# Heads and weight products as loops in a decode kernel (attention over a K/V cache, mixed with a gated MLP)

## The chip, the cores and the metric

One core of a Trainium2 chip. The metric is the device time of one execution in microseconds (us), lower is better. Engine names: PE is the matrix engine (PEld its weight loads), DVE the vector engine, ACT the scalar engine, POOL or GpSimd the general engine, SP the engine that issues the large transfers. PEldq, SPq and the like are rows of an engine's instruction queue: register, branch, semaphore and transfer-issuing instructions.

## The reference

All data is bfloat16. One token `x` (512 values) goes two ways, and a scalar gate mixes the results:

```python
x = A_x                                             # [1, 1, 512]
g = sigmoid((x * gate_w).sum(-1))
q = (x @ wq).reshape(32 heads, 128)                 # wq [512, 4096]
scores = einsum(q, k_cache) * 128 ** -0.5           # k_cache [1, 32, 65536, 128]
p = softmax(scores)
o = einsum(p, v_cache)                              # v_cache [1, 32, 65536, 128]
a = o.reshape(4096) @ wo                            # wo [4096, 512]
b = (silu(x @ w_gate) * (x @ w_up)) @ w_down        # F = 1792
out = g * a + (1 - g) * b
```

K and V are 2 x 32 x 16.8 MB; with the weights 1087.8 MB are read.

## The kernel before, in words

The program is written engine by engine: each engine's block is a list of instructions in program order, and semaphores tie the engines together (`wait_ge(s, n)` holds an engine until semaphore `s` has reached `n`). Nothing is planned at run time.

**Memory.** One large tile `mem` holds the weights, K and V in kilobyte places. Each half of a head's K or V (z = 0 or 1, 8.39 MB) has a fixed place; `load(kind, h, z)` fetches it with one transfer. Head 0's second K half takes the place of wq, so it waits for the last product with wq (`s_q`); the first two loads for head 1 and V of head 0 wait on `ktdone` (and `s_b`), which count transposes and the last product with w_down. SP issues all large transfers in program order on one queue.

**Start.** PE turns `x` into a column (`xTb`), multiplies it with wq for 32 heads (L446: four products of 128x128 weights per head, each with one column), then DVE and ACT spread q into `qd`, `qcur` and the gate into `gcol`. PE then forms gate and up (`mlp_up`, L474: 14 columns j, eight products each), ACT and DVE form `guT`, and PE starts `psY` with w_down (L482). DVE's first transposes (`transposes(0)`, L336) stand behind `guT` in its program, PE's first scores behind L482.

**Heads.** For each head DVE transposes K in 16 pieces into two buffers of `kt`; PE multiplies each with `qcur` (`scores`, L462) into `psS` and raises `qkdone`; a transpose waits until the piece two before it has been used. After the 16th, DVE takes the maximum, GpSimd reduces it over partitions (L280), ACT forms the exponentials (L305, L307) and copies the next head's query (L310), GpSimd sums (L282), DVE reorders them into `pb`, and PE multiplies with V (L515) during the next head, raising `pvdone`, which frees V's places for SP. `row_norm` on ACT scales the finished row and `turn` on PE stands it up as a column of `oTn`. PE and DVE run the heads as loops (`Fori`) already; PE's scores are inner loops (L508) whose output address `psS[:, ds(j * (2 * PR) + o, 4)]` is in a register. ACT, SP and GpSimd have the 32 heads written out.

**End.** The last V comes in eight pieces (`tail`), behind wo. PE multiplies the first piece (`piece(0)`, 128 rows), brings the first 31 heads' outputs into `oR` (L554), folds them with wo into `psY` (L559, 31 products), then does piece 1 (128 rows), the start of `psZ` (L567), pieces 2 to 7 (256 rows in all), and the last head's part of wo (L583). ACT copies the result (L314) and it is written out.

The lines of the products that the change turns into loops are

```python
last = nc.tensor.matmul(psM[:, 128 + h:129 + h], wq_ap[:, c, h * Dh:(h + 1) * Dh], xTb[:, c:c + 1], ...)
last = nc.tensor.matmul(psM[:, o + j:o + j + 1], w[:, c, :, j], xTb[:, c:c + 1], ...)
last = nc.tensor.matmul(psW[:, 0:1], vt[:, r * Dh:(r + 1) * Dh], pb[:, col:col + 1], ...)
last = nc.tensor.matmul(psY[0:1, :], oR[:, j:j + 1], wo_ap[:, j, :], start=False, stop=(j == 30))
```

Of the kernel before, what the change touches and what calls it, by code (L numbers as in the profile page):

```python
# [5 lines left out]
P = 128  # L6
# [9 lines left out]
ds = bass.DynSlice  # L16
# [5 lines left out]
def bass_gated_mix__mha_block_cached__swiglu_ffn__decode_kernel(  # L22
# [13 lines left out]
    _, H, S, Dh = A_k_cache.shape  # L36
    D = A_wq.shape[0]
    F = B_w_gate.shape[1]
    Dc = D // P
    FC = F // P  # L40
    R = S // P
    HR = R // 2
    NP = HR // PR
# [5 lines left out]
    KA, KZ, VA, VZ, V0 = 32, 0, 120, 96, 96  # L49
# [15 lines left out]
    with ExitStack() as ctx:  # L65
# [6 lines left out]
        def sem(name):  # L72
            return ctx.enter_context(nc.semaphore(name))
# [3 lines left out]
        psY = psum("psY", [P, 512], F32)  # L77
# [31 lines left out]
        def at(kb, n):  # L109
            return mem[:, kb * KB:kb * KB + n]  # L110
# [39 lines left out]
        pvdone = sem("pvdone")  # L150
        s_mx = sem("s_mx")
        s_ar = sem("s_ar")
        s_nb = sem("s_nb")
        expdone = sem("expdone")
        s_pba = sem("s_pba")
# [40 lines left out]

        def place(kind, h, z):
            if kind == "k":
                return (KA, V0)[z] if h == 0 else (KA, KZ)[z]
            return (VA, VZ)[z]  # L200

        def kv_dram(cache, h):
            return cache[0, h].rearrange("(b p r) d -> b p (r d)", b=2, p=P)

        for n, kb in (("wq", WQ), ("wg", WG), ("wu", WU), ("wd", WD)):
            src = w_dram[n]
# [7 lines left out]
        @block.sync  # L214
        def _(sp):
            def load(kind, h, z):
                cache = A_k_cache if kind == "k" else A_v_cache
                sp.dma_start(at(place(kind, h, z), HR * Dh), kv_dram(cache, h)[z]).then_inc(d[kind + "az"[z]], 16)

            half = HR // 2 * Dh  # L220
            for n in range(2):
                sp.dma_start(at(KA + 32 * n, half), kv_dram(A_k_cache, 0)[0][:, n * half:n * half + half]).then_inc(
                    (d["ka0"], d["ka"])[n], 16)
            sp.wait_ge(s_q, 1)
            load("k", 0, 1)
            for h in range(1, H):
                sp.wait_ge(ktdone, 2 * NP * h - 4 if h > 1 else NP)
                load("k", h, 0)
                if h == 1:
                    sp.wait_ge(ktdone, 2 * NP - 3)  # L230
                    sp.wait_ge(s_b, 1)
                else:
                    sp.wait_ge(pvdone, 4 * h - 1)
                load("v", h - 1, 0)
                sp.wait_ge(ktdone, 2 * NP * h + NP // 2)
                load("k", h, 1)
                sp.wait_ge(pvdone, 4 * h + 1)
                load("v", h - 1, 1)
            sp.wait_ge(ktdone, 2 * NP * H - NP)
            sp.dma_start(at(WO, 31 * D), w_dram["wo"][:, 0:31 * D]).then_inc(d["wo"], 16)  # L240
            src = A_v_cache[0, H - 1].rearrange("(b p r) d -> b p (r d)", b=2, p=P)
            need = {0: (ktdone, 2 * NP * H - 4), 1: (ktdone, 2 * NP * H), 2: (pvdone, 4 * H - 1)}
            for n, (kb, r0, nr) in enumerate(tail):
                if n in need:
                    sp.wait_ge(*need[n])
                b, o = divmod(r0, HR)
                sp.dma_start(at(kb, nr * Dh), src[b][:, o * Dh:(o + nr) * Dh]).then_inc(dt_[n], 16)  # L247
            sp.wait_ge(pvdone, 4 * H)
            sp.dma_start(at(WOJ, D), wj_dram).then_inc(d["wj"], 16)
            sp.dma_start(at(WO31, D), w31_dram).then_inc(d["w31"], 16)  # L250
            sp.wait_ge(s_fin, 1)
            sp.dma_start(out_dram[2:4, :], fin[32:34, :]).then_inc(s_out2, 16)

        @block.gpsimd
        def _(pool):
            nc.gpsimd.memset(onesf[0:1, :], 1.0)
            nc.gpsimd.memset(sel, 0.0).then_inc(s_sel0, 1)
            pool.wait_ge(s_sel0, 1)
            for je in range(4):
                off = 64 * (je // 2) + je % 2  # L260
                v = sel[:, je, :].rearrange("p (g d) -> p g d", g=4)
                last = nc.gpsimd.affine_select(out=v, in_=v, compare_op=ALU.not_equal, fill=1.0, base=-off,
                                               pattern=[[0, 4], [-2, 32]], channel_multiplier=1)
            last.then_inc(s_sel, 1)
            nc.gpsimd.memset(unit[:], 0.0).then_inc(s_unit0, 1)
            pool.wait_ge(s_unit0, 1)
            nc.gpsimd.affine_select(out=unit[:], in_=unit[:], compare_op=ALU.not_equal, fill=1.0, base=0,
                                    pattern=[[-1, 4]], channel_multiplier=1).then_inc(s_unit, 1)
            nc.gpsimd.memset(bmat[:], 0.0).then_inc(s_b0, 1)
            for q in range(4):  # L270
                pool.wait_ge(s_b0, q + 1)
                nc.gpsimd.affine_select(out=bmat[:], in_=bmat[:], compare_op=ALU.not_equal, fill=1.0, base=-32 * q,
                                        pattern=[[-1, 32]], channel_multiplier=1).then_inc(s_b0, 1)
            nc.gpsimd.memset(hot[0:1, :, :], 0.0).then_inc(s_hot0, 1)
            pool.wait_ge(s_hot0, 1)
            nc.gpsimd.affine_select(out=hot[0:1, :, :], in_=hot[0:1, :, :], compare_op=ALU.not_equal, fill=1.0,
                                    base=0, pattern=[[1, 2], [-1, 2]], channel_multiplier=0).then_inc(s_hot, 1)
            for h in range(H):
                pool.wait_ge(s_mx, h + 1)
                nc.gpsimd.partition_all_reduce(amx, mxs, P, RMAX).then_inc(s_ar, 1)  # L280
                pool.wait_ge(expdone, h + 1)
                nc.gpsimd.partition_all_reduce(Lt, rsum, P, RADD).then_inc(s_L, 1)  # L282

        @block.scalar
        def _(act):
# [8 lines left out]

            def row_norm(h):
                act.wait_ge(s_li, h + 1)
                act.wait_ge(pvdone, 4 * h + 8)
                act.wait_ge(s_pt, h + 1)
                nc.scalar.mul(orow[0:4, :], psO[0:4, :], Li[0:4, :]).then_inc(s_or, 1)  # L299
                act.wait_ge(s_pt, h + 2)  # L300
                nc.scalar.mul(oTn[:, h:h + 1], psT[:, 0:1], gcol[:, 0:1]).then_inc(s_otn, 1)  # L301

            for h in range(H):
                act.wait_ge(s_ar, h + 1)
                nc.scalar.mul(nbias, amx, -SCALE).then_inc(s_nb, 1)  # L305
                act.wait_ge(s_nb, h + 1)
                nc.scalar.activation(pa[:], psS[:], ACT.Exp, bias=nbias, scale=SCALE,  # L307
                                     accum_out=rsum).then_inc(expdone, 1)
                if h < H - 1:
                    nc.scalar.copy(qcur[:], qd[:, h + 1, :, :]).then_inc(s_qc, 1)  # L310
                if h >= 1:
                    row_norm(h - 1)
            act.wait_ge(s_z4, 1)
            nc.scalar.copy(fin[0:34, :], psZ[0:34, 0:128]).then_inc(s_fin, 1)  # L314
            act.wait_ge(s_fin, 1)
# [119 lines left out]
        def _(pe):  # L435
# [5 lines left out]
            last.then_inc(s_xT, 1)  # L441
            pe.wait_ge(s_xTb, 1)
            pe.wait_ge(d["wq"], 16)
            for h in range(H):
                for c in range(Dc):
                    last = nc.tensor.matmul(psM[:, 128 + h:129 + h], wq_ap[:, c, h * Dh:(h + 1) * Dh],  # L446
                                            xTb[:, c:c + 1], start=(c == 0), stop=(c == Dc - 1))
            last.then_inc(s_q, 1)
            pe.wait_ge(s_qTb, 1)
            pe.wait_ge(s_sel, 1)  # L450
# [16 lines left out]
            def mlp_up():  # L467
                pe.wait_ge(s_gc, 1)
                pe.wait_ge(d["wg"], 16)
                pe.wait_ge(d["wu"], 16)  # L470
                for j in range(FC):
                    for w, o in ((wg_ap, 64), (wu_ap, 80)):
                        for c in range(Dc):
                            last = nc.tensor.matmul(psM[:, o + j:o + j + 1], w[:, c, :, j], xTb[:, c:c + 1],  # L474
                                                    start=(c == 0), stop=(c == Dc - 1))
                last.then_inc(s_h, 1)

            mlp_up()
            pe.wait_ge(d["wd"], 16)
# [58 lines left out]
            def piece(n):  # L538
                kb, r0, nr = tail[n]
                pe.wait_ge(dt_[n], 16)  # L540
                vt = at(kb, nr * Dh)
                for r in range(nr):
                    col = k_col[r0 + r]
                    last = nc.tensor.matmul(psW[:, 0:1], vt[:, r * Dh:(r + 1) * Dh], pb[:, col:col + 1],  # L544
                                            start=(r0 + r == 0), stop=(r0 + r == R - 1))
                return last

            pe.wait_ge(s_or, H)
# [6 lines left out]
                             start=True, stop=True).then_inc(s_R, 1)  # L555
            pe.wait_ge(s_oR, 1)
            pe.wait_ge(d["wo"], 16)
            for j in range(31):
                last = nc.tensor.matmul(psY[0:1, :], oR[:, j:j + 1], wo_ap[:, j, :], start=False, stop=(j == 30))  # L559
            last.then_inc(s_y, 1)  # L560
            piece(1)
            pe.wait_ge(s_yr, 1)
# [51 lines left out]
```

## Time and profile before

| what | value |
|---|---|
| median of 3 runs (lowest, highest) | 2518.57 us (2518.57, 2519.21) |
| the profiled execution's own time | 2518.66 us |
| its span, first to last instruction | 2517.4 us |
| busy: PE, DVE, ACT, POOL | 67%, 56%, 3%, 1% |
| granted PE clock, mean | 0.71 of full speed |
| read from memory | 1087.77 MB, 432 GB/s over the span |
| instruction fetch in the page's queues q8 and q14 | 9 packets, 0.15 MB; 5 packets, 0.04 MB |

The page cuts the span into 40 slices; its row GB/s is what the transfers moved in each. The trace's timeline gives start, duration, engine, line, what is written from what, the count of merged instructions, and in brackets the idle time of the engine before them and what ended it. A source view gives, for one line, the durations (least, median, greatest, in ns) and the first and last start.

### The profile page before, as it was taken

How to read it: one execution, taken by the hardware profiler on the slowest of the kernel's cores; microseconds unless marked ns; L12 is line 12 of the kernel's file. 1: busy time of each engine (PE TensorE's matmuls, PEld its weight loads, DVE VectorE, ACT ScalarE, POOL GpSimd, SP SyncE). 2: the span in 40 equal slices, each digit the busy share in tenths (PEclk: the TensorE clock that was granted, in tenths of full speed). 3: DMA queues.
4: the chain of work that ended last, by engine and by line, in shares of the span. 5: the costliest groups of instructions: out<-in, count | busy, mean ns of one | idle time of the engine just before them, and what ended most of it. 6: DMA issues, size and time to landing. Idle time of an engine off the chain costs nothing.

```text
span 2517.4 us, 50622 instructions
## 1 busy us (share of the span) xinstructions
PE 1675.3 (67%) x21432; PEld 956.8 (38%) x21432; DVE 1397.7 (56%) x1631; ACT 65.6 (3%) x195; POOL 26.8 (1%) x83
## 2 busy tenths in 40 slices
PE   4566756667666577566676666766657756667667
PEld 3333333333433334333333333343333433333334
DVE  3764565554655645646456555465464564644653
ACT  0000000000000000000000000000000000000000
POOL 0000000000000000000000000000000000000000
PEclk8667767677677677676776767767767767677677
DMA  9999999999999999999999999999999999999999
GB/s 418 433 433 434 435 433 433 434 433 433 433 433 433 433 433 433 433 433 433 433 435 432 434 433 434 433 434 433 434 433 433 433 433 434 433 433 433 433 434 396
DMA packets 20474, 1087.97 MB, mean 432 GB/s; under 512 B 2282, under 2 KB 2668, under 8 KB 2924
## 3 DMA queue, kind: packets, MB, share of 16 engines
q1 hardware_dynamic: 20452, 1087.78, 99.9%
q8 instruction: 9, 0.15, 0.0%
q14 instruction: 5, 0.04, 0.0%
q10 hardware_dynamic: 8, 0.00, 0.0%
HBM read 1087.77 MB, written 0.00 MB: 432 GB/s over the span
## 4 chain that ended last, share of the span: by engine, by line
DMA 72%; PE 27%; DVE 0%; issue 0%; SPq 0%; ACT 0%
DMA mem<-in_A_v_cache_dram 70%; PE psO L515 27%; DMA mem<-in_A_k_cache_dram 2%; DMA mem<-in_A_wq_dram 1%; DVE kt L336 0%; PE psM L446 0%; SPq L247 0%; PE psZ L583 0%; PE psW L544 0%; ACT fin L314 0%
## 5 line engine op out<-in xcount | busy, mean ns | idle before, releaser
L462 PE MATMUL psS<-qcur,kt 128*128 128x4 bf16 x16384 | 573.7, 169 | 776.4 <-DVE kt L405 458.4
L515 PE MATMUL psO<-mem,pb 128*4 128x512 bf16 x3968 | 1033.6, 428 | 35.2 <-DMA mem<-in_A_v_cache_dram 35.2
L405 DVE STREAM_TRANSPOSE kt<-mem 128x2048 uint32<-128x2048 uint32 x248 | 551.2, 2280 | 571.9 <-DMA mem<-in_A_k_cache_dram 571.0
L462 PEld LDWEIGHTS psS<-qcur,kt 128*128 128x128 bf16 x16384 | 534.7, 106 | 852.4 <-issue 850.0
L412 DVE STREAM_TRANSPOSE kt<-mem 128x2048 uint32<-128x2048 uint32 x248 | 547.6, 2274 | 407.6 <-DMA mem<-in_A_k_cache_dram 407.6
L515 PEld LDWEIGHTS psO<-mem,pb 128*4 128x4 bf16 x3968 | 361.2, 93 | 666.2 <-issue 235.7
L345 DVE COPY pb<-pa 32x64 bf16<-32x64 bf16 x1024 | 233.5, 228 | 24.2 <-PE psO L515 9.5
L350 DVE TENSOR_REDUCE sm<-psS 128x1 f32<-128x512 f32 x32 | 22.1, 692 | 42.3 <-PE psS L462 42.3
L336 DVE STREAM_TRANSPOSE kt<-mem 128x2048 uint32<-128x2048 uint32 x16 | 35.4, 2277 | 16.9 <-DMA mem<-in_A_k_cache_dram 16.9
L280 POOL PARTITION_ALL_REDUCE sm<-sm x32 | 11.2, 351 | 2392.6 <-DVE sm L350 2392.6
L301 ACT ACTIVATE oTn<-psT,gcol 128x1 bf16<-128x1 f32 x31 | 8.2, 263 | 1063.2 <-PE psT L489 1063.2
L489 PE MATMUL psT<-unit,orow 4*128 4x1 f32 x256 | 33.5, 248 | 0.8 <-ACT orow L299 0.8
L299 ACT ACTIVATE orow<-psO,sm 4x512 f32<-4x512 f32 x31 | 21.0, 677 | 439.5 <-issue 439.5
L489 PEld LDWEIGHTS psT<-unit,orow 4*128 4x128 f32 x256 | 30.8, 186 | 1.9 <-ACT orow L299 1.3
L305 ACT ACTIVATE sm<-sm 128x1 f32<-128x1 f32 x32 | 6.5, 203 | 886.3 <-POOL sm L280 886.3
L307 ACT ACTIVATE pa<-psS,sm 128x512 bf16<-128x512 f32 x32 | 22.0, 687 | 1.0
L544 PE MATMUL psW<-pb,mem 128*128 128x1 bf16 x512 | 14.6, 165 | 7.6 <-DMA mem<-in_A_v_cache_dram 7.1
L544 PEld LDWEIGHTS psW<-pb,mem 128*128 128x128 bf16 x512 | 14.1, 102 | 8.7 <-issue 6.5
L282 POOL PARTITION_ALL_REDUCE sm<-sm x32 | 12.3, 383 | 36.4 <-ACT pa L307 36.4
L446 PE MATMUL psM<-xTb,mem 128*128 128x1 bf16 x128 | 3.6, 165 | 11.1 <-DMA mem<-in_A_wq_dram 11.1
L474 PE MATMUL psM<-xTb,mem 128*128 128x1 bf16 x112 | 6.9, 198 | 4.9 <-DMA mem<-in_B_w_up_dram 4.9
L432 DVE TENSOR_SCALAR w<-psW,sm 128x2 bf16<-128x2 f32 x1 | 0.2, 221 | 16.5 <-PE psW L544 16.5
(64 smaller groups left out, 63.1 us busy)
## 6 DMA issues: line engine op xcount, KB each, us to landing
mem<-in_A_v_cache_dram SPq DMA_DIRECT2D x3, 4096.0 KB, 29.4
mem<-in_A_k_cache_dram SPq DMA_DIRECT2D x2, 4096.0 KB, 38.8
mem<-in_A_wq_dram SPq DMA_DIRECT2D x1, 4096.0 KB, 12.6
mem<-in_A_wo_dram SPq DMA_DIRECT2D x1, 3968.0 KB, 37.0
mem<-in_A_v_cache_dram SPq DMA_DIRECT2D x1, 2048.0 KB, 32.9
mem<-in_B_w_gate_dram SPq DMA_DIRECT2D x1, 1792.0 KB, 16.4
mem<-in_B_w_up_dram SPq DMA_DIRECT2D x1, 1792.0 KB, 21.3
mem<-in_B_w_down_dram SPq DMA_DIRECT2D x1, 1792.0 KB, 25.1
```

Of the source, the lines that this page charges most:

```text
L282: nc.gpsimd.partition_all_reduce(Lt, rsum, P, RADD).then_inc(s_L, 1)
L299: nc.scalar.mul(orow[0:4, :], psO[0:4, :], Li[0:4, :]).then_inc(s_or, 1)
L307: nc.scalar.activation(pa[:], psS[:], ACT.Exp, bias=nbias, scale=SCALE, accum_out=rsum).then_inc(expdone, 1)
L336: nc.vector.transpose(kt[:, i % 2, :].rearrange("p (j r t) -> p r j t", j=2, t=32), src.rearrange("p (r j t) -> p r j t", j=2, t=32)).then ...
L345: last = nc.vector.tensor_copy(dst, sr)
L350: nc.vector.reduce_max(mxs, psS[:], AX_X).then_inc(s_mx, 1)
L405: nc.vector.transpose(kt[:, c % 2, :].rearrange("p (j r t) -> p r j t", j=2, t=32), src.rearrange("p (r j t) -> p r j t", j=2, t=32)).then ...
L412: nc.vector.transpose(kt[:, c % 2, :].rearrange("p (j r t) -> p r j t", j=2, t=32), src.rearrange("p (r j t) -> p r j t", j=2, t=32)).then ...
L462: last = nc.tensor.matmul(psS[:, o:o + 4] if j is None else psS[:, ds(j * (2 * PR) + o, 4)], ktb[b][:, je // 2, r, :, je % 2], qcur[:, je, ...
L489: last = nc.tensor.matmul(psT[:, 0:1], orow[0:4, i * Dh:(i + 1) * Dh], unit[0:4, i:i + 1], start=(i == 0), stop=(i == 3))
L515: last = nc.tensor.matmul(psO[0:4, :], pb[:, k_col[256 * z + r]:k_col[256 * z + r] + 4], vt[:, r * Dh:(r + 4) * Dh], start=(z == 0 and par ...
L544: last = nc.tensor.matmul(psW[:, 0:1], vt[:, r * Dh:(r + 1) * Dh], pb[:, col:col + 1], start=(r0 + r == 0), stop=(r0 + r == R - 1))
```

## The change

The 32 heads of SP, ACT and GpSimd, which were written out, become hardware loops: SP keeps head 1's loads and loops over 30 heads; ACT keeps the first exponentials and the last head and loops over 30; GpSimd loops over all 32, with an increment of a new semaphore `s_pool` between each wait and its reduction. K and V are then addressed in memory by a register. On PE four groups of products become loops: wq (7 turns of 4 heads, 4 heads written out), gate and up (13 turns of one column, the last written out), the first piece of the last V (8 rows written out, 15 turns of 8), and the fold with wo (5 turns of 5, 6 written out). In these loops the addresses of weights, columns and outputs come from registers (`ds(...)`). No product, transfer or buffer is added or left out.

```diff
         def kv_dram(cache, h):
-            return cache[0, h].rearrange("(b p r) d -> b p (r d)", b=2, p=P)
+            if isinstance(h, int):
+                return cache[0, h].rearrange("(b p r) d -> b p (r d)", b=2, p=P)
+            return cache[0, ds(h, 1)].rearrange("a (b p r) d -> b (a p) (r d)", b=2, p=P)
...
-            for h in range(1, H):
-                sp.wait_ge(ktdone, 2 * NP * h - 4 if h > 1 else NP)
-                load("k", h, 0)
-                if h == 1:
-                    sp.wait_ge(ktdone, 2 * NP - 3)
-                    sp.wait_ge(s_b, 1)
-                else:
-                    sp.wait_ge(pvdone, 4 * h - 1)
-                load("v", h - 1, 0)
-                sp.wait_ge(ktdone, 2 * NP * h + NP // 2)
-                load("k", h, 1)
-                sp.wait_ge(pvdone, 4 * h + 1)
-                load("v", h - 1, 1)
+            sp.wait_ge(ktdone, NP)
+            load("k", 1, 0)
+            sp.wait_ge(ktdone, 2 * NP - 3)
+            sp.wait_ge(s_b, 1)
+            load("v", 0, 0)
+            sp.wait_ge(ktdone, 2 * NP + NP // 2)
+            load("k", 1, 1)
+            sp.wait_ge(pvdone, 5)
+            load("v", 0, 1)
+            with nc.sync.Fori(0, H - 2) as i:
+                sp.wait_ge(ktdone, i * (2 * NP) + (4 * NP - 4))
+                load("k", i + 2, 0)
+                sp.wait_ge(pvdone, i * 4 + 7)
+                load("v", i + 1, 0)
+                sp.wait_ge(ktdone, i * (2 * NP) + (4 * NP + NP // 2))
+                load("k", i + 2, 1)
+                sp.wait_ge(pvdone, i * 4 + 9)
+                load("v", i + 1, 1)
...
-            for h in range(H):
+            with nc.gpsimd.Fori(0, H) as h:
                 pool.wait_ge(s_mx, h + 1)
+                nc.gpsimd.sem_inc(s_pool, 1)
                 nc.gpsimd.partition_all_reduce(amx, mxs, P, RMAX).then_inc(s_ar, 1)
                 pool.wait_ge(expdone, h + 1)
+                nc.gpsimd.sem_inc(s_pool, 1)
                 nc.gpsimd.partition_all_reduce(Lt, rsum, P, RADD).then_inc(s_L, 1)
...
-                nc.scalar.mul(oTn[:, h:h + 1], psT[:, 0:1], gcol[:, 0:1]).then_inc(s_otn, 1)
-
-            for h in range(H):
+                nc.scalar.mul(oTn[:, ds(h, 1)], psT[:, 0:1], gcol[:, 0:1]).then_inc(s_otn, 1)
+
+            def exps(h):
                 act.wait_ge(s_ar, h + 1)
...
-                if h < H - 1:
-                    nc.scalar.copy(qcur[:], qd[:, h + 1, :, :]).then_inc(s_qc, 1)
-                if h >= 1:
-                    row_norm(h - 1)
+
+            exps(0)
+            nc.scalar.copy(qcur[:], qd[:, 1, :, :]).then_inc(s_qc, 1)
+            with nc.scalar.Fori(0, H - 2) as i:
+                exps(i + 1)
+                nc.scalar.copy(qcur[:], qd[:, ds(i + 2, 1), :, :].rearrange("p a e g -> p (a e) g")).then_inc(s_qc, 1)
+                row_norm(i)
+            exps(H - 1)
+            row_norm(H - 2)
...
-            for h in range(H):
+
+            def project(h):
                 for c in range(Dc):
-                    last = nc.tensor.matmul(psM[:, 128 + h:129 + h], wq_ap[:, c, h * Dh:(h + 1) * Dh],
+                    last = nc.tensor.matmul(psM[:, ds(h + 128, 1)], wq_ap[:, c, ds(h * Dh, Dh)],
                                             xTb[:, c:c + 1], start=(c == 0), stop=(c == Dc - 1))
+                return last
+
+            with nc.tensor.Fori(0, (H - 4) // 4) as i:
+                for h in range(4):
+                    project(i * 4 + h)
+            for h in range(H - 4, H):
+                last = project(h)
...
-                for j in range(FC):
+                def up(j):
                     for w, o in ((wg_ap, 64), (wu_ap, 80)):
                         for c in range(Dc):
-                            last = nc.tensor.matmul(psM[:, o + j:o + j + 1], w[:, c, :, j], xTb[:, c:c + 1],
-                                                    start=(c == 0), stop=(c == Dc - 1))
-                last.then_inc(s_h, 1)
+                            last = nc.tensor.matmul(psM[:, ds(j + o, 1)],
+                                                    w[:, c, :, ds(j, 1)].rearrange("p m a -> p (m a)"),
+                                                    xTb[:, c:c + 1], start=(c == 0), stop=(c == Dc - 1))
+                    return last
+
+                with nc.tensor.Fori(0, FC - 1) as j:
+                    up(j)
+                up(FC - 1).then_inc(s_h, 1)
...
+                def row(r, col):
+                    return nc.tensor.matmul(psW[:, 0:1], vt[:, ds(r * Dh, Dh)], pb[:, ds(col, 1)],
...
+                if n == 0:
+                    first = 8
+                    for r in range(first):
+                        row(r, k_col[r])
+                    with nc.tensor.Fori(0, nr // 8 - 1) as i:
+                        for r in range(8):
+                            row(i * 8 + (first + r), i * 8 + (first + r))
+                    return
                 for r in range(nr):
-                    col = k_col[r0 + r]
...
+                    last = row(r, k_col[r0 + r])
                 return last
...
-            for j in range(31):
-                last = nc.tensor.matmul(psY[0:1, :], oR[:, j:j + 1], wo_ap[:, j, :], start=False, stop=(j == 30))
+
+            def fold(j, stop):
+                return nc.tensor.matmul(psY[0:1, :], oR[:, ds(j, 1)],
+                                        wo_ap[:, ds(j, 1), :].rearrange("p a n -> p (a n)"), start=False, stop=stop)
+
+            with nc.tensor.Fori(0, 5) as i:
+                for j in range(5):
+                    fold(i * 5 + j, False)
+            for j in range(25, 31):
+                last = fold(j, j == 30)
             last.then_inc(s_y, 1)
```

## The prediction

> **What bounds the kernel now.** I read the page first, for what is full.
>
> ```profile
> span 2517.4 us, 50622 instructions
> ...
> GB/s 418 433 433 434 435 433 433 434 433 433 433 433 433 433 433 433 433 433 433 433 435 432 434 433 434 433 434 433 434 433 433 433 433 434 433 433 433 433 434 396
> ...
> q1 hardware_dynamic: 20452, 1087.78, 99.9%
> ```
>
> One queue keeps 16 DMA engines busy for 99.9% of the span, at one rate; no compute engine passes 67% (PE). The trace's DMA records show the first packet at 1.75 us and the last input packet at 2514.81 us, with no hole between. So the bytes set the time, and an edit costs only if it empties that queue or lengthens what runs before the first or after the last byte. I therefore asked what covers each load: SP's line for the loads in the loop.
>
> ```profile
> L218 SPq DMA_DIRECT2D mem<-in_A_k_cache_dram x63: 327/328/328, 17.1 to 2417.0; - x63
> ...
> DMA to landing us min/median/max: 26.9/29.6/48.9
> ```
>
> A load is 8.39 MB: 19.4 us at 433 GB/s. The shortest way from issue to landing is 26.9, so at least 7.5 us of older work lies queued ahead of every load. That is the cover of the steady state. Next the two ends, by the timeline. The start, in three cuts of it (PE, DVE, SP's issue):
>
> ```profile
> 13.48 3.55 PE L446 MATMUL psM<-xTb,mem 128*128 128x1 bf16 x128 [11.10 <-DMA mem<-in_A_wq_dram]
> ...
> 23.04 6.85 PE L474 MATMUL psM<-xTb,mem 128*128 128x1 bf16 x112 [4.92 <-DMA mem<-in_B_w_up_dram]
> 31.42 5.02 PE L482 MATMUL psY<-mem,guT 128*1 128x512 bf16 x14 [1.53 <-DVE guT L389]
> ```
>
> ```profile
> 36.95 8.89 DVE L336 STREAM_TRANSPOSE kt<-mem 128x2048 uint32<-128x2048 uint32 x4 [5.67 <-DMA mem<-in_A_k_cache_dram]
> ...
> 66.00 11.08 DVE L336 STREAM_TRANSPOSE kt<-mem 128x2048 uint32<-128x2048 uint32 x5 [10.46 <-DMA mem<-in_A_k_cache_dram]
> ```
>
> ```profile
> 55.56 0.33 SPq L218 DMA_DIRECT2D mem<-in_A_k_cache_dram  x1
> ```
>
> And the end, PE alone:
>
> ```profile
> 2485.32 3.51 PE L544 MATMUL psW<-pb,mem 128*128 128x1 bf16 x128 [2.02 <-DMA mem<-in_A_v_cache_dram]
> ...
> 2489.16 8.61 PE L559 MATMUL psY<-mem,oR 128*1 128x512 bf16 x31 [0.28 <-DVE oR L426]
> 2497.71 3.36 PE L544 MATMUL psW<-pb,mem 128*128 128x1 bf16 x128
> ...
> 2504.77 3.55 PE L544 MATMUL psW<-pb,mem 128*128 128x1 bf16 x128 [3.17 <-DMA mem<-in_A_v_cache_dram]
> ```
>
> At the start DVE has 5.67 us to spare before its first transpose. The issue at 55.56 (k of head 1) waits for the eighth transpose (ktdone 8), and the queue is dry when the load before it lands at 66.0. At the end PE starts the last V's first piece when it lands (2485.3) and meets waits of a few us. What PE does from there in order, run end to end, is: 0.3 to the fold, 8.6, 3.3, 0.6 (L567), 3.5, then 124 products at 27 ns, 3.4: 19.7, with some 0.4 for its waits 20.1. The last V product now ends at 2514.93, so the first piece may last 2514.93 - 2485.3 - 20.1 = 9.5 us before the end moves; it lasts 3.5.
>
> **What a looped product costs.** PE already has such loops (L508, L462), and the trace has their register instructions:
>
> ```profile
> L462 PEldq FUSED_REGOPS  x3584: 46/46/65, 39.3 to 2465.4; - x200
> ```
>
> ```profile
> L508 PEldq COMPARE_BRANCH  x224: 76/208/243, 42.6 to 2465.6; - x112
> ```
>
> 3584 is a quarter of the 14,336 looped score products: each distinct register address takes one instruction, and the four products of a row share theirs. The new products share less: a row of the last V's piece has two addresses of its own (vt, pb), a head of wq has five (four weight slices, one output), one j of gate and up has ten. From the starts of records in the loop: a register instruction and its four weight loads and four matmuls take 124 ns; the first weight load starts 96 ns after the register instruction; two register instructions in a row are 99 ns apart (L508 to L501). So a product with one register instruction costs at least 46 + 2 x (124-46)/8 = 66 ns, at most 96 + 2 x 28/8 = 103 ns. I take 90, nearer the upper end, because that 96 ns is seen directly and how many of the 124 ns the eight others take is not. With two: 112 to 202; I take 99 + 90, 190 ns. An unlooped product: 27 ns (3.51/128). A loop's turn: increment to branch 93, branch to next instruction 267, that first register instruction 99: 0.46 us (0.36 if the last is counted among the addresses).
>
> **The change, part by part.** *The last V's first piece*: 8 unlooped rows 0.2, 120 rows x 0.19 = 22.8, 15 turns x 0.46 = 6.9: 29.9 us (19.0 to 33, the upper with 14 ns more for the longer address, by the 60 ns records of L462's first rows). Cover 9.5: the end moves by 20.4 (9.5 to 23.5). *Fold with wo*: five products take PE 5 x 0.278 = 1.39, the sequencer 5 x 0.19 + 0.46 = 1.41: hidden but for 0.1 (0 to 0.5 at 0.2 each). If PE's queue doesn't run ahead, 2 more.
>
> *wq*: 28 heads x (190 + 3 x 90 = 460 ns) = 12.9, 7 turns 3.2, four heads unlooped 0.4: 16.5 us (11.6 to 17.9) for 3.55. It ends at 30.0 (25.1 to 31.4). SP waits there on s_q to issue head 0's second K half: harmless, since the load ahead lands at 46.65 (DVE's wait on it ends there). DVE and ACT take 2.7 from s_q to gcol as before (17.06 to 19.73): PE is at gate and up at 32.7 (27.8 to 34.1), where it now comes at 23.04 by a DMA. *Gate and up*: one j is 2 x 460 = 920 ns plus 0.46; 13 of them 17.9, one unlooped 0.5: 18.4 us (13.2 to 19.8) for 6.85. Ends at 51.1 (41.0 to 53.9). guT follows 1.4 later, 52.5: past 36.95, so DVE's 5.67 us of cover is gone, its first transposes start there, and PE's 5.2 us of psY come before the first scores: 57.7, first group done at 58.9, when DVE may write kt again; six transposes at 2.22 follow: the eighth ends at 72.2 (62.1 to 75.0). SP's issue moves from 55.56 to there, bytes flow 1.0 later (first issue 0.72, first packet 1.75): the queue is dry from 66.0 to 73.2, **7.2 us** (0 to 10). What comes next is timed by landings and only shifts.
>
> *SP, ACT and GpSimd loops*: no loop of theirs is in this trace. PE's and DVE's register instructions (0.1 us apart) and turns are the nearest rows. Of what each repeats per head, the turn falls into long idle times (GpSimd's 75 us, ACT's 28 before L305), and the addresses between an SP wait and its issue, three or four, are 0.4 us; on SP the next load's wait is queued behind. ACT's chain (L305, L307) and GpSimd's two added semaphore steps together delay the exponentials by under 2 us; s_pool's increments stand behind waits that the reductions had before, with only the reduction behind them. All is under 7.5 us of cover: 0. *Instruction fetch*: the page's nine packets of q8 take 1.0 to 1.1 us each in the DMA records, q14's five in the span 0.31: 11 us of one engine, 0.7 us of sixteen. Perhaps a third goes: -0.3 (0 to -0.7).
>
> **Sum**, on the profiled execution's 2518.66 (span 2517.4 and 1.26 around it; 0.09 above the median): +20.4 +0.1 +7.2 -0.3 = 2546.1. Lower bounds together 2528, upper 2553.
>
> **Rivals.** *Not slower: register work costs a mere slot.* Place: the last V's piece. If an instruction costs the group's average, 124/9 = 13.8 ns, a row is 55 ns, the piece 0.2 + 6.6 + 6.9 = 13.7, 4.2 over its cover; wq then takes 8.7, gate and up 12.8 (the array's 61 ns a product hide the addresses), the eighth transpose ends near 59, no hole: 2522.6. It decides at (9.5 + 5.3 - 0.2 - 6.9)/120 = 64 ns a row for staying within 0.2%. For it: only 17 ns are lost per row of scores. Against: the 96 and 99 ns. Chance 0.10. The Trainium skill's "Runtime: NRT & Kernel Launch" (Instruction fetch mechanics) names one issue floor, about 20 cycles per instruction, which would favour this rival and its 2522.6; the trace's 99 ns between two register instructions speaks against applying it to them.
>
> *Every back edge refetches its code.* Forty new turns on PE, 20 at each end, at a packet's 1.05 us or more: 42 on top, 2588. Against: branch to next instruction is 265 to 312 ns in nine of ten of 160 inner turns, and q8 fetched nothing between 90 and 2491 us, with all of the heads' loops in between. 0.04. The same page and section has a taken branch outside a two-page window wait for a fetch, which is this rival's mechanism; here the bodies are short, and the trace shows it nowhere.
>
> *SP's, ACT's or GpSimd's loop eats more than 7.5 us per half head*: at 10, 2.5 x 30 or more, past 2593. Nothing in the profile is so slow. 0.03. *The loops end up without register work* (addresses folded): 2518.4. Two looped addresses cannot be constants; 0.03. *Faster*: needs 5 us of DMA time that no row offers; 0.02.
>
> **Numbers.** My sum holds 0.78. Range 2521 to 2558: from the slot rival's time past the upper bounds, with 5 us for the loops that no row shows. Slower by over 0.2% 0.85 (sum, refetch, slow loops), within 0.2% 0.13, faster 0.02; 0.2%, 5 us, is about what a measurement of this kernel can tell from no change.
>
> **What would show it.** Right: some 240 register instructions on the V piece's line and about 30 us of it from 2492 on (2485.3 plus the hole); no DMA wait of PE after that piece; the k issue of head 1 after 66 us and a lower second GB/s slice; q1's share below 99.9%; issue to landing still 27 us or more later. Wrong: the V piece under 15 us, k issued before 65, or holes in the DMA in the middle of the span.

## The result and the profile after

The changed kernel takes 2563.25 us (median of 6 runs, 2562.64 to 2563.88) against 2519.02: a ratio of 1.0176, interval 1.0166 to 1.0186, 44 us slower. The direction and the two places of the loss were forecast; the size was not: 2546 was said, with 2558 as the upper end.

The page of the changed kernel, the lines that answer to those of before:

```profile
span 2562.5 us, 52097 instructions
...
GB/s 413 328 426 437 431 434 434 434 434 434 433 434 434 433 435 432 435 432 436 431 437 428 440 428 440 428 438 430 437 431 437 431 436 432 435 433 434 434 429 213
...
q1 hardware_dynamic: 20452, 1087.78, 98.2%
q8 instruction: 7, 0.11, 0.0%
q14 instruction: 1, 0.01, 0.0%
```

The bytes are the same. Only the second slice (328 GB/s) and the last (213) have lost; from the third to the last but one the queue is as full as it was. So there is no loss per head. Each slice is 64 us: (433 - 328)/433 of it is 15.5 us, and (396 - 213)/433 is 27 us. In the DMA records the queue stands empty from 64.86 to 79.48 us, and the last input packet ends at 2532.1, 28 us before the last V product. The hole costs more than the 14.6 us in which all 16 engines stand still: their last packets before it end one after another, between 63.7 and 64.9 us, and in the first steps of 2 us after 80 us the queue moves 339 and 397 GB/s. By the bytes moved (at 27 MB) the changed kernel is then 16.1 us behind the kernel before.

The start, in the timelines of PE, DVE and SP (start us, us, engine, line, operation; in brackets the idle time before and its cause; "..." stands for lines left out):

```profile
14.13 2.52 PE L462 MATMUL psM<-xTb,mem 128*128 128x1 bf16 x16 [11.63 <-DMA mem<-in_A_wq_dram]
17.12 2.53 PE L462 MATMUL psM<-xTb,mem 128*128 128x1 bf16 x16 [0.48 <-issue]
...
31.98 3.19 PE L462 MATMUL psM<-xTb,mem 128*128 128x1 bf16 x32 [0.45 <-issue]
...
38.14 1.15 PE L497 MATMUL psM<-xTb,mem 128*128 128x1 bf16 x8 [1.88 <-ACT gcol L301]
39.60 1.17 PE L497 MATMUL psM<-xTb,mem 128*128 128x1 bf16 x8 [0.32 <-issue]
...
55.90 1.84 PE L497 MATMUL psM<-xTb,mem 128*128 128x1 bf16 x16 [0.31 <-issue]
59.27 5.03 PE L510 MATMUL psY<-mem,guT 128*1 128x512 bf16 x14 [1.53 <-DVE guT L404]
```

```profile
59.03 4.50 DVE L351 STREAM_TRANSPOSE kt<-mem 128x2048 uint32<-128x2048 uint32 x2
65.22 30.82 DVE L351 STREAM_TRANSPOSE kt<-mem 128x2048 uint32<-128x2048 uint32 x14 [1.69 <-PE psS L485]
```

```profile
78.52 0.33 SPq L221 DMA_DIRECT2D mem<-in_A_k_cache_dram  x1
```

wq's 128 products now take 21.0 us (14.13 to 35.17), one turn of four heads 2.99. Gate and up take 19.6 (38.14 to 57.74), one j 1.47. DVE's first transposes no longer wait for a DMA but for guT, the third waits for PE, and the issue for head 1's first K half, at 55.56 before, comes at 78.52, behind the eighth transpose.

The end, PE alone:

```profile
2502.36 2.31 PE L572 MATMUL psW<-pb,mem 128*128 128x1 bf16 x16 [1.74 <-DMA mem<-in_A_v_cache_dram]
2505.14 1.93 PE L572 MATMUL psW<-pb,mem 128*128 x8 [0.47 <-issue]
...
2536.71 1.92 PE L572 MATMUL psW<-pb,mem 128*128 x8 [0.46 <-issue]
2538.82 0.18 PE L595 MATMUL psQ<-bmat,amat 128*128 128x32 bf16 x1 [0.19 <-issue]
2539.60 9.27 PE L601 MATMUL psY<-mem,oR 128*1 x31 [0.59 <-DVE oR L441]
2548.80 3.41 PE L572 MATMUL psW<-pb,mem 128*128 128x1 bf16 x128
...
2553.08 6.99 PE L572 MATMUL psW<-pb,mem 128*128 128x1 bf16 x256
```

The first piece starts 17.0 us later than before and lasts 36.3 us (2502.36 to 2538.63) for 3.5. After it PE never waits for a DMA: all later pieces run in one row, x256. The last V product ends at 2560.07, 45.1 us later: 17.0 from the start, 26.8 by which the piece passes its cover of 9.5, and 1.3 in the fold, the pause before it and psZ.

What a looped row is made of is in the source view of the piece (durations least, median, greatest in ns):

```profile
L572 PEldq FUSED_REGOPS  x120: 46/74/84, 2502.6 to 2538.2; - x120
L572 PEldq ALU_OP  x105: 32/32/36, 2502.9 to 2538.4; - x105
```

Two register instructions a row, as assumed (FUSED_REGOPS and ALU_OP are both such; with 15 on the loop's own line L581 they are 240 for 120 rows). By the starts of records, the second follows 132 ns after the first, the weight load 60 later, the next row's first register instruction 53 after that: 245 ns a row. In wq's loop a product with one register instruction takes 124: 96 to its weight load, 28 or 29 on to the next. Gate and up is different from what was assumed:

```profile
L497 PEldq FUSED_REGOPS  x91: 46/46/79, 38.2 to 56.7; - x91
L502 PEldq FUSED_REGOPS  x13: 78/78/78, 38.0 to 55.8; - x13
```

That is 104 for 13 columns: eight register instructions a column, one for each product, where ten addresses had been counted. Some instructions last 78 or 79 ns instead of 46; the first product of each half, whose output address is new, has one of these and no second instruction.

### The profile page after: what moved, and what is told of

Read it like the earlier page. It is cut to its first block, busy times and chain, and to the rows that moved or that the text cites. A ratio compares the mean times of both kernels' runs of the same rounds, so it can differ in the third digit from the quotient of the medians.

```text
span 2562.5 us, 52097 instructions
## 1 busy us (share of the span) xinstructions
PE 1707.5 (67%) x21432; PEld 976.5 (38%) x21432; DVE 1397.3 (55%) x1631; ACT 65.6 (3%) x195; POOL 26.8 (1%) x83
## 4 chain that ended last, share of the span: by engine, by line
DMA 71%; DVE 14%; issue 10%; PE 4%; SPq 0%; DVEq 0%; ACT 0%; POOL 0%; ACTq 0%; POOLq 0%
DMA mem<-in_A_k_cache_dram 69%; DVE kt L420 7%; DVE kt L427 6%; PE psW L572 1%; DMA mem<-in_A_v_cache_dram 1%; DVE kt L351 1%; PE psO L543 1%; PE psM L462 1%; PE psM L497 1%; DMA mem<-in_A_wq_dram 1%; PE psY L601 0%; PE psS L485 0%; PE psY L510 0%; SPq L221 0%; DVE pb L360 0%
## 5 line engine op out<-in xcount | busy, mean ns | idle before, releaser
L485 PEld LDWEIGHTS psS<-qcur,kt 128*128 128x128 bf16 x16384 | 529.0, 105 | 849.3 <-issue 846.8
L572 PE MATMUL psW<-pb,mem 128*128 128x1 bf16 (+1 forms) x512 | 30.6, 165 | 17.8 <-issue 6.9
L289 POOL PARTITION_ALL_REDUCE sm<-sm x32 | 11.2, 351 | 2406.1 <-DVE sm L365 2313.5
L311 ACT ACTIVATE oTn<-psT,gcol 128x1 f32 (+1 forms) x31 | 8.2, 263 | 1070.0 <-PE psT L517 1070.0
L572 PEld LDWEIGHTS psW<-pb,mem 128*128 128x128 bf16 (+1 forms) x512 | 22.9, 102 | 26.2 <-issue 14.4
L462 PE MATMUL psM<-xTb,mem 128*128 128x1 bf16 x128 | 16.5, 181 | 16.2 <-DMA mem<-in_A_wq_dram 11.6
L462 PEld LDWEIGHTS psM<-xTb,mem 128*128 (+1 forms) x128 | 12.2, 104 | 20.5 <-issue 18.4
L497 PE MATMUL psM<-xTb,mem 128*128 128x1 bf16 x112 | 15.7, 216 | 5.8 <-issue 3.9
```

The costliest lines, as they stand in the source:

```text
L462: last = nc.tensor.matmul(psM[:, ds(h + 128, 1)], wq_ap[:, c, ds(h * Dh, Dh)], xTb[:, c:c + 1], start=(c == 0), stop=(c == Dc - 1))
L485: last = nc.tensor.matmul(psS[:, o:o + 4] if j is None else psS[:, ds(j * (2 * PR) + o, 4)], ktb[b][:, je // 2, r, :, je % 2], qcur[:, je, ...
L497: last = nc.tensor.matmul(psM[:, ds(j + o, 1)], w[:, c, :, ds(j, 1)].rearrange("p m a -> p (m a)"), xTb[:, c:c + 1], start=(c == 0), stop= ...
L572: return nc.tensor.matmul(psW[:, 0:1], vt[:, ds(r * Dh, Dh)], pb[:, ds(col, 1)], start=(isinstance(r, int) and r0 + r == 0), stop=(isinsta ...
```

## Experiments

All are edits of the changed kernel, against the kernel before in the same runs (2518.8 us). Theory A: the loss is what PE's register-addressed products take beyond their cover at the two ends. The rivals look for it in the other engines' loops, in code fetch, or in products and register instructions adding up.

**The V piece written out (x1_tail_plain).**

```diff
-                if n == 0:
+                if n < 0:
                     first = 8
```

> The changed kernel with the last V's first piece written out again (its 128 products as before); all other loops stay. Theory A (the loss is the price of register-addressed products at the two ends, 17.0 us at the start and 27 to 28 at the end): the start's 17.0 us stay, the end is back, 2519 + 17 = 2536 us (2535 to 2537.5), and the fold's loop stays hidden. Rival B (part of the loss comes from the loops of SP, ACT and GpSimd, such as GpSimd's first reduction, which starts 10.3 us after its wait): the start's share is theirs, the same 2536 here, but then the next run would not return to the time of before. Rival C (the end is late because code is fetched late after a loop, not because of the rows): the end would stay 3 us or more late, above 2539.

Measured: 2536.56 us (2536.30 to 2537.82), 17.7 over before. PE at the end:

```profile
2502.12 3.55 PE L572 MATMUL psW<-pb,mem 128*128 128x1 bf16 x128 [0.84 <-DMA mem<-in_A_v_cache_dram]
...
2506.32 9.63 PE L601 MATMUL psY<-mem,oR 128*1 x31 [0.60 <-DVE oR L441]
...
2521.70 3.39 PE L572 MATMUL psW<-pb,mem 128*128 128x1 bf16 x122 [0.35 <-DMA mem<-in_A_v_cache_dram]
```

The end is back to waits on the DMA, with the fold's loop in place. The DMA stands empty from 64.8 to 80.2 us, 15.4 us (14.6 in the full change). So 26.7 us of the 44 hang on this one loop; late code is not what holds the end.

**wq, gate and up written out (x2_start_plain).**

```diff
-            with nc.tensor.Fori(0, (H - 4) // 4) as i:
-                for h in range(4):
-                    project(i * 4 + h)
-            for h in range(H - 4, H):
+            for h in range(H):
                 last = project(h)
...
-                with nc.tensor.Fori(0, FC - 1) as j:
+                for j in range(FC - 1):
                     up(j)
```

> The changed kernel with wq's and gate's and up's products written out again; SP's, ACT's and GpSimd's loops, the V piece's loop and the fold's loop stay. Theory A: no hole in the DMA at the start; 2519 + 27.5 = 2546.5 us (2545.5 to 2548). Rival B: GpSimd's first reduction 10 us late holds the first loads of head 1 back: a hole of 2 to 10 us near 100 to 125 us, 2549 to 2557.

Measured: 2549.31 us (2548.42 to 2550.58). The hole at 65 us is gone, but the time lies 2.8 above theory A, in the rival's range. GpSimd's first reduction stands at 95.03 us (85.84 before) and the issue of head 1's second K half at 102.58 (94.52), as the rival has it. The queue is nowhere wholly empty, but it moves only 290 GB/s between 102 and 104 us and 172 between 124 and 126.

**All of PE written out (x3_pe_plain).** Both edits above, and the fold:

```diff
-            with nc.tensor.Fori(0, 5) as i:
-                for j in range(5):
-                    fold(i * 5 + j, False)
-            for j in range(25, 31):
+            for j in range(31):
                 last = fold(j, j == 30)
```

> All four groups of PE's products written out again; only the loops of SP, ACT and GpSimd stay. Theory A: they lie under the cover of the loads, 2519 us (2518 to 2520.5), at most 1 us for GpSimd's late first reduction. Rival B: 2521 to 2530, with a hole near 105 us or with issues of SP less than 19.4 us before landing.

Measured: 2523.17 us (2521.43 to 2526.39; ratio 1.0018, interval 1.0008 to 1.0027). Theory A fails here as it stood: the loops of SP, ACT and GpSimd are not free. The queue runs empty near 104.5 and 125.3 us, for 0.4 and 0.7 us; most of the loss is in the thin stretches around these moments. By the bytes moved the kernel is 2.0 us behind the kernel before after the first (at 45 MB) and 4.8 after the second (at 53 MB). The timelines of GpSimd, DVE and SP show from where; first the lines of the kernel before:

```profile
85.84 0.38 POOL L280 PARTITION_ALL_REDUCE sm<-sm  x1 [69.78 <-DVE sm L350]
```

```profile
94.52 0.33 SPq L218 DMA_DIRECT2D mem<-in_A_k_cache_dram  x1
```

And x3_pe_plain:

```profile
96.33 0.38 POOL L289 PARTITION_ALL_REDUCE sm<-sm  x1 [79.85 <-issue]
```

```profile
85.16 0.69 DVE L365 TENSOR_REDUCE sm<-psS 128x1 f32<-128x512 f32 x1 [1.34 <-PE psS L482]
85.76 4.50 DVE L420 STREAM_TRANSPOSE kt<-mem 128x2048 uint32<-128x2048 uint32 x2
99.34 4.51 DVE L420 STREAM_TRANSPOSE kt<-mem 128x2048 uint32<-128x2048 uint32 x2 [9.08 <-PE psS L482]
```

```profile
103.88 0.33 SPq L221 DMA_DIRECT2D mem<-in_A_k_cache_dram  x1
```

Head 0's maximum is ready at 85.85, but GpSimd reduces it at 96.33 (85.84 before). ACT's exponentials and its copy of head 1's query follow, PE's scores of head 1 wait for that copy, DVE's third transpose of head 1 waits 9.08 us for PE, and SP issues head 1's second K half at 103.88 instead of 94.52, when its cover is used up. GpSimd's row says "issue", not DVE: it was not waiting for the maximum any more. In the records its two MODIFY_POOL_CONFIG steps, which stood at 16.3 us before, now come right behind the wait (86.3 us here, the reduction 10.0 later; 98.5 and 10.3 in the full change). In the heads that follow, the reduction starts 0.2 to 0.3 us after its wait: the long gap is the first head's alone. What GpSimd does in it no record shows.

**The other half: PE's loops alone (x4_pe_loops).** SP, ACT and GpSimd as before.

```diff
-            with nc.gpsimd.Fori(0, H) as h:
+            for h in range(H):
                 pool.wait_ge(s_mx, h + 1)
-                nc.gpsimd.sem_inc(s_pool, 1)
                 nc.gpsimd.partition_all_reduce(amx, mxs, P, RMAX).then_inc(s_ar, 1)
...
-            with nc.sync.Fori(0, H - 2) as i:
+            for h in range(1, H):
...
-            with nc.scalar.Fori(0, H - 2) as i:
+            for h in range(H):
```

> The other half: SP, ACT and GpSimd written out as before, PE's four loops as in the change. Theory A: 2563 us (2561.5 to 2563.5). Rival B: 5 to 10 us less, 2553 to 2558, since the other engines' loops carry part of the loss.

Measured: 2562.21 us (2562.07 to 2563.34). Of the 44 us, 43 are PE's. The loops of the small engines cost 4.3 us alone (x3_pe_plain) and about 1 on top of PE's, by medians whose ranges of runs overlap: the 10 us of GpSimd's first reduction fall behind a start that is late already.

**One register address a row (x5_one_address).**

```diff
-                            row(i * 8 + (first + r), i * 8 + (first + r))
+                            row(i * 8 + (first + r), first + r)
```

> The changed kernel, but in the looped rows of the last V's piece the column of pb is a fixed one (the eight of the first eight rows, in every turn), so a row has one register address instead of two; the last head's product therefore weighs those rows wrongly. Theory A (each register instruction sets a fixed time, about 96 ns to the weight load and 28 more to the next register instruction): a row goes from 245 to about 140 ns, the piece from 36.5 to about 24.5 us, 2551 us (2549.5 to 2553). The prediction's price of 90 ns a row: 18 us for the piece, 2545 us.

Measured: 2551.53 us (2551.09 to 2551.81), 11.7 less than the full change. The source view and PE's timeline:

```profile
L572 PEldq FUSED_REGOPS  x105: 64/64/79, 2502.8 to 2526.6; - x105
```

```profile
2519.18 1.20 PE L572 MATMUL psW<-pb,mem 128*128 128x1 bf16 x8 [0.43 <-issue]
2520.85 1.18 PE L572 MATMUL psW<-pb,mem 128*128 128x1 bf16 x8 [0.47 <-issue]
```

A row takes 142 ns by the records and a turn of eight 1.63 to 1.67 us where it took 2.4; the piece ends at 2526.9. The prediction's price of 90 ns a row would have given 2545.

**Every looped product twice (x6_twice).**

```diff
                             row(i * 8 + (first + r), i * 8 + (first + r))
+                            row(i * 8 + (first + r), i * 8 + (first + r))
```

> The changed kernel with every looped product of the last V's piece issued twice with the same two register addresses (120 products more, the sum counts those rows twice). Theory A: the second product falls into the time that the register instructions take anyway: 0 to 0.5 us more, 2563 to 2564. The prediction's price (products and register instructions add up, 7 to 27 ns a product): 0.8 to 3.2 us more, 2564 to 2566.5.

Measured: 2563.87 us (2563.10 to 2564.47) beside 2563.25 (2562.64 to 2563.88): 0.6 more, the two ranges of runs overlap, and it lies just outside A's 0.5. The timeline decides it better:

```profile
2517.20 1.93 PE L572 MATMUL psW<-pb,mem 128*128 x16 [0.43 <-issue]
2519.56 1.97 PE L572 MATMUL psW<-pb,mem 128*128 x16 [0.43 <-issue]
2521.96 1.95 PE L572 MATMUL psW<-pb,mem 128*128 x16 [0.43 <-issue]
```

Sixteen products take the 2.4 us that eight took. By the starts of register instructions a row takes 254.8 ns in the mean, 254.6 in the changed kernel (the median is 245 in both). The second product fits beside the register instructions.

**Only wq's loop, or only gate's and up's (x7_wq_loop, x8_gate_loop).** Both keep the loops of SP, ACT and the fold, with GpSimd and the V piece written out.

```diff
-                if n == 0:
+                if n < 0:
...
-                with nc.tensor.Fori(0, FC - 1) as j:
+                for j in range(FC - 1):
                     up(j)
```

is x7; x8 has wq's loop written out in place of these last lines:

```diff
-            with nc.tensor.Fori(0, (H - 4) // 4) as i:
-                for h in range(4):
-                    project(i * 4 + h)
-            for h in range(H - 4, H):
+            for h in range(H):
                 last = project(h)
```

> Of PE's loops only wq's and the fold's stay (gate and up and the V piece written out), SP's and ACT's loops stay, GpSimd is written out. Theory A with covers: wq ends at 35.2, gate and up 38.1 to 45.0, guT 46.4, first scores at 51.7 to 52.9, the eighth transpose 13.3 later at 66.2, the first bytes at 67.2 to 67.3 against a queue that runs dry at 64.9: a hole of 2.3 us, 2521.3 us (2520.3 to 2522.5). Rival (each loop costs its share of the 17.0 us in proportion to the time that it adds, 17.5 of 30): 10 us, 2529.

> The same with gate's and up's loop instead of wq's. Theory A with covers: gate and up 23.0 to 42.6, guT 44.0, first scores at 49.3 to 50.5, the eighth transpose at 63.8, first bytes at 64.8 against a queue that runs dry at 64.9: no hole, 2519 us (2518.5 to 2519.8). Rival (proportional share, 12.8 of 30): 7 us, 2526.

Measured: wq alone 2521.73 us (2521.09 to 2522.30), gate and up alone 2520.35 (2519.21 to 2521.35; ratio 1.0006, interval 0.9996 to 1.0015). With wq's loop the issue stands at 65.98 us and the queue is empty from 65.56 to 66.94. The time lies in the range that was given, but with a hole of 1.4 us for the 2.3 expected, so the reckoning was right only in part. The time with gate's loop lies 0.5 us above its range. There the issue stands at 63.45, and the profiled execution (span 2518.4 us) has no moment at which all engines stand still; by the bytes moved it falls 1.1 us behind at this very place all the same (at 27 MB; with wq's loop 3.6). The sixteen shares of the older load end between 63.6 and 65.5 us, and between 64 and 67 us the queue moves 243, 358 and 360 GB/s. So "no hole" was not "no loss": the cover ends where the first engine runs out, here some 2 us before the last one does. Proportional shares (10 and 7 us) are excluded: 2.9 and 1.6 alone, 17 together.

**SP's and ACT's loops alone (x9_sp_act).** As x3_pe_plain, with GpSimd written out:

```diff
-            with nc.gpsimd.Fori(0, H) as h:
+            for h in range(H):
                 pool.wait_ge(s_mx, h + 1)
-                nc.gpsimd.sem_inc(s_pool, 1)
```

> Only SP's and ACT's loops stay; PE's four groups and GpSimd are written out as before. Theory A2 (what the three small engines' loops cost, 2.5 to 7.5 us, is GpSimd's alone: its wait is now an instruction of its own, the switch to the code of the reduction comes behind it instead of 70 us ahead, and the first reduction starts 10 us late): 2518.8 us (2518.4 to 2519.3), head 1's second K issue back from 103.9 to 94.5 us. Rival B2 (SP's or ACT's loop costs it): 2521 to 2524, as with all three.

Measured: 2518.75 us (2518.32 to 2519.36) beside 2518.80; ratio 1.0000, interval 0.9991 to 1.0009. The issue is back at 94.69.

**All three loops, GpSimd's first head taken out (x10_first_head_out).** An edit of x3_pe_plain.

```diff
-            with nc.gpsimd.Fori(0, H) as h:
+            pool.wait_ge(s_mx, 1)
+            nc.gpsimd.partition_all_reduce(amx, mxs, P, RMAX).then_inc(s_ar, 1)
+            pool.wait_ge(expdone, 1)
+            nc.gpsimd.partition_all_reduce(Lt, rsum, P, RADD).then_inc(s_L, 1)
+            with nc.gpsimd.Fori(1, H) as h:
```

> All three loops of SP, ACT and GpSimd stay, PE written out, but GpSimd's first head is taken out of its loop, with the waits on the reductions themselves as before. Theory A2: the switch happens early in the wait, 2518.8 us (2518.3 to 2519.3). Rival C2 (the added semaphore steps of every head cost it): 2521 to 2524 still. If the fetches of code that the loops save count (five of 0.3 us on one of 16 engines), it is at most 0.1 us under the kernel before, not measurable.

Measured: 2518.60 us (2518.30 to 2518.81); ratio 0.9999, interval 0.9990 to 1.0008. GpSimd's and SP's timelines:

```profile
85.96 0.38 POOL L287 PARTITION_ALL_REDUCE sm<-sm  x1 [68.74 <-DVE sm L369]
```

```profile
94.64 0.33 SPq L221 DMA_DIRECT2D mem<-in_A_k_cache_dram  x1
```

The first reduction is on time again, now released by DVE, and its two MODIFY_POOL_CONFIG steps stand at 17.4 us. So SP's, ACT's and GpSimd's loops cost nothing except through that first wait. Whether the separate wait or the added increment matters is not told apart: the two are one record, and every run has both or neither in the first head. No version beats the kernel before by more than the runs scatter.

## Why the prediction was wrong, point by point

**Right in mechanism:** the DMA queue bounds the time; the steady state covers the new loops of SP and ACT (least issue to landing 26.8 us with both loops alone, 26.7 with all three in x10; in the full change 22.9 among the early loads, 26.8 from 150 us on); the loss sits in a hole before head 1's first K half and in the last V's first piece; the fold hides. It took 0.66 us more than before, but its time goes with the granted clock of its stretch, looped or not: 8.36 us at 0.82 (x10) and 9.56 at 0.71 (x3) written out, 9.27 at 0.73 (full change) and 9.78 at 0.69 (x7) looped; time times clock is 6.7 to 6.9 us in each. Only the pause before it is longer with the loop, 0.6 us for 0.3.

**The term that failed: the price of a looped product.** The step took the 124 ns of a score group as one register instruction (46 ns by the lower bound, the 96 to the first weight load by the upper) plus eight others that share the rest, and gave a lone product two of the eight shares. They don't share it: the register instruction alone sets the 124. A second product beside it is free (x6), and without three others a lone product still takes 124. With one address a product takes 124 to 142, outside the bounds of 66 to 103; with two a row takes 245, outside 112 to 202. The upper bound was no bound, since it let the seven nanoseconds of two dispatched instructions stand for the whole way from the weight load to the next register instruction, which is 28 in the very records that were quoted, and took 99 ns between two register instructions where the longer ones of the new loops (74 to 79 ns each) are 132 to 137 apart.

| term | forecast | measured |
|---|---|---|
| row with two addresses, one address | 190, 90 ns | 245, 124 to 142 ns |
| V piece, end moved by it | 29.9, 20.4 us | 36.3, 26.8 us |
| fold, the pause before it and psZ | 0.1 us | 1.3 us |
| wq; a head of it | 16.5 us; 460 ns | 21.0 us; about 650 ns |
| gate and up; one j with its turn | 18.4, 1.38 us | 19.6, 1.47 us |
| register instructions in one j; ns for each | 10; 92 | 8; about 129 |
| eighth transpose and issue | 72.2 us | 78.5 us |
| hole in the DMA; the loss at the start | 7.2, 7.2 us | 14.6, 17.0 us |
| SP, ACT and GpSimd | 0 | 4.3 alone, about 1 here (within the 17.0) |
| instruction fetch | -0.3 us | not told apart from 0 (x10) |

The misses add up: 6.4 in the V piece, 1.2 around the fold, 9.8 at the start and 0.3 of fetch are 17.7, and the profiled execution (2563.88 us) lies 17.8 above the forecast of 2546.1. That one j of gate and up came near its forecast is luck: two register instructions too many were counted, each priced too low ((1.47 - 0.44)/8 = 0.129 us).

**The hole's edges** are a second, smaller miss: the queue was taken to run dry when the load's landing was seen before (66.0), but in the changed run its last packet ends at 64.86, so the hole is 1.1 us longer on that side. Part of this is the way from the last packet to the landing, 0.45 us in both runs (65.53 to 65.98 before, 64.86 to 65.31 in the changed run); why the load itself ends 0.7 us earlier stays open (in x7 it ends at 65.56). On top come the thin stretches on both sides of the hole. The cover of the steady state was taken too large too: of the 7.5 us, 1.0 go from issue to the first packet and 0.45 from the last packet to the landing, which leaves an estimated 6. The chain in between (guT, psY, first scores, six transposes at 2.2 us) ran as written; it began 0.65 us later, with wq's products.

**GpSimd** was put at 0 because its wait is long, and because "only the reduction" was said to stand behind the increments. What was missed is what else stands there: before, the wait was on the reduction, and the two MODIFY_POOL_CONFIG steps ran 70 us ahead; with the wait as an instruction of its own they run behind it, and the first reduction starts 10 us later. x3_pe_plain against x10_first_head_out shows what that costs: 4.6 us.

**The rivals:** the "mere slot" rival at 2522.6 needed 64 ns a row and is out by a factor of almost four. "Every back edge refetches" is out: the page shows seven packets on q8 for nine before, and a turn costs about 0.44 us over its rows (2.4 - 8 x 0.245). A slow loop of SP or ACT is out (x9). Loops without register work are out: the V piece has 240 register instructions.

## What to carry to other kernels

Price a looped product by its register instructions, read as the distance from one to the next in an existing loop of the same kind. Count how many addresses of its own each product has, and check the count in a trace where there is one: two addresses were two instructions in the V piece and one in gate and up. Products that share an address cost as much as one (four in the scores, two in x6). Then hold the sum against the cover of the stage where the loop stands, and end that cover where the first DMA engine runs out: two loops that cost 2.9 and 1.6 us alone (the second with an interval that reaches down to nothing) cost 17 together, because the first microseconds of each went into the same cover. When a wait becomes an instruction of its own, look at what the engine used to do ahead of it.

## What the runs showed that was not expected

On PE one register instruction of 46 ns holds the way to the next product for 96 ns and the way to the next register instruction for 124, whether one product (wq) or four (scores) follow; one of 64 ns takes 142 (x5), and two before one product take 245. On GpSimd 10.0 to 10.3 us lay between the second MODIFY_POOL_CONFIG step and the first reduction (x3, full change), and where the wait was an instruction of its own these steps came only after it. A queue that is about to run dry loses time before it is empty and after it is filled again: 1.1 us with no empty moment at all (x8). A load's last packet ended 0.45 us before its landing was signalled.
